# Gates by Silu with the last tile in column halves, and two chunks' row factors spread by DMA

## The chip, the cores and the metric

The kernel runs on one core of a Trainium2 chip. A core has five engines that run side by side, each with its own queue of instructions in order: TensorE (PE, matmuls), VectorE (DVE), ScalarE (ACT, activation functions from a loaded table), GpSimd (POOL) and SyncE (SP, which here only issues DMAs). TensorE writes to PSUM, eight banks of 2 KB for each of 128 partitions; the other data lie in SBUF. The metric is the device time of one execution in microseconds (us). Times inside an execution count from the start of its span, which is the time from the first to the last instruction.

## The reference

The input `x` is 2048 tokens by 512 features. All of it is computed on `xn`, the layer norm of `x`:

```python
xn = _layernorm(x)
s = _A_ref(xn, A_wqkv, A_wo)                  # windowed attention
g = _silu(_B_ref(xn, B_w1, B_w2, B_w3, B_w4))  # a mixer and an MLP
return x + s * g
```

- `_A_ref`: `q`, `k`, `v` for 32 heads of 16; token `i` attends to the eight tokens `i, i-2, ..., i-14`; softmax, weighted sum, then `@ wo`.
- `_B_ref`: `h = gelu(layernorm(xn) @ w1)`, four quarters of its columns shifted by 1, -1, 2 and -2 tokens, `@ w2`, added to `xn` as `x1`; then `x1 + gelu(layernorm(x1) @ w3) @ w4`, with 1376 hidden features.

The layer norm inside `_B_ref` is taken of `xn`, which is already normalised: its mean is zero, and it only multiplies each token by a factor, `(var * rstd**2 + eps) ** -0.5`. These are the row factors. `silu(g)` is `g * sigmoid(g)`, which equals `0.5 * g * (1 + tanh(g / 2))`.

## The kernel before

Tokens are sorted by parity, `p` = 0 (even) and 1 (odd), 1024 each, since attention with dilation 2 stays inside a parity. Each parity has two chunks of 512 tokens, so chunks 0 and 1 are parity 0, chunks 2 and 3 parity 1. A chunk has four tiles of 128 tokens, and tile `t` counts from 0 to 15. Most of SBUF is one arena, cut by hand into buffers that take turns.

The order of every engine's instructions is the order of the program's text: it is written out by hand (`manual_schedule`), and each engine's queue runs in that order. Work goes in these stages:

1. Up to about 46 us: layer norm of each chunk (`ln_stats`, `ln_norm`), its transpose (`stage_t` by TensorE for chunks 0, 1 and 3; `turn_dma` for chunk 2, a store to DRAM whose returned function issues the transposing load), the q and k projections (`qk_pair`, `qk_one`), and `stage_w1` for `h`. The moving operand of `stage_w1(c, ...)` is `xn2T[c]`, the transposed chunk times its row factors.
2. To 88 us: attention of parity 0 in units of 120 queries (`attend`: `scores`, `values`, `weighted`), with the `w2` tiles between.
3. To 126 us: `w3` with Gelu.
4. To 172 us: attention of parity 1, with the `w4` tiles of parity 0, their gates and final tiles between.
5. To the end: for each tile `t` of parity 1 a `w4_tile` (11 matmuls), its gate, and a `final_tile` one behind (4 matmuls with `wo`, times the gate, plus `x`), then stores.

**Row factors.** `ln_again(c)` computes them, a column of one value for each token with tokens on partitions: four small multiplies and an add (L345 to L347), on GpSimd except for chunk 3, and a power of -0.5 on GpSimd (L350). `stage_w1` needs them along the free axis, the same on all partitions. `stage_r(c)` does that on TensorE: four matmuls (L382) of the broadcast column with the identity, into one PSUM bank, which ScalarE copies (L386) to the last quarter of `xn2T[c]`. `stage_m(c)` (L392, VectorE) multiplies the transposed chunk by it in place. `xn2T` has two buffers, for even and odd chunks.

**PSUM.** Tags `s`, `t`, `o` have two banks each and are taken in turn by `psa`; `w` and `b` have one each, in turn by `psb`, whose counter is `cnt["b"]`. `first_t` and `stage_t` name `w` or `b` themselves. A matmul into a bank waits until the engine that reads it out is done.

**Masks and spreads.** `mask_full`, `mask_fill` (L241, L251, VectorE) write the mask's rows into the buffers of keys and queries; `spread` (L261) copies the heads' rows in by DMA, 32 of them on SP's queue from 27.88 to 50.9 us. SP's queue issues in order, and a DMA that waits holds those behind it.

**Gate and final tile.** `w4_tile` ends with an add of PSUM to `xn` on VectorE (L549). `gate(t)` is a Tanh on ScalarE (L558, `scale=0.5`) and on VectorE `(tanh + 1) * x` (L559). The missing factor 0.5 is in the attention: `v_aug` has columns of 2.0 that give twice the softmax denominator. `final_tile` multiplies PSUM by the gate (L713) and adds `x` (L715); for the tile before the last, with `act=True`, ScalarE first copies PSUM to SBUF (L712). Tables of activation functions are loaded ahead by name (`preload_act_table_set`).

Of the kernel before, what the change touches and what calls it, by code (L numbers as in the profile page):

```python
# [8 lines left out]
AF = mybir.ActivationFunctionType  # L9
ALU = mybir.AluOpType  # L10
BF16 = mybir.dt.bfloat16
# [4 lines left out]
def kernel(  # L16
# [14 lines left out]
    nc = tc.nc  # L31
    P = 128
    S = 2048
    D = 512
# [79 lines left out]
    rr_at = (184, 75)  # L114
    sg_at = (61, 66, B0 + 33.5)

    cnt = {"v": 0, "p": 0, "b": 0, "r": 0, "g": 0}

    def pst(tag, name):
        return psum.tile([P, 2 if tag in "sto" else 1, CH], F32, name=name, tag=tag)  # L120
# [209 lines left out]
    def ln_norm(c, part=slice(None)):  # L330
        p, k = c // 2, c % 2
        x_c = xn[p][:, k * TPC : (k + 1) * TPC, :]
        for lo, hi, mv, rstd in lns[c][part]:
            for j in range(lo, hi):
# [2 lines left out]
                    scalar2=rstd[:, j - lo : j - lo + 1], op0=ALU.subtract, op1=ALU.mult,  # L337
                )

    def ln_again(c):  # L340
        r2 = small.tile([P, TPC], F32, name="r2", tag="r2")
        eng = nc.vector if c == 3 else nc.gpsimd
        for lo, hi, mv, rstd in lns[c]:
            r = r2[:, lo:hi]
            eng.tensor_tensor(out=r, in0=rstd, in1=rstd, op=ALU.mult)  # L345
            eng.tensor_tensor(out=r, in0=r, in1=mv[:, :, 1], op=ALU.mult)
        eng.tensor_scalar(out=r2, in0=r2, scalar1=EPS, scalar2=None, op0=ALU.add)  # L347
        r2b = small.tile([P, TPC], BF16, name="r2b", tag="r2b")
        with nc.allow_low_precision("bf16 factors"):
            nc.gpsimd.tensor_tensor(out=r2b, in0=r2, in1=nhalf, op=ALU.pow)  # L350
# [181 lines left out]
    def w4_tile(t):  # L532
        c, jj = t // TPC, t % TPC
        p, i = c // 2, (c % 2) * TPC + jj
        st = {}

        def half(lo, hi):
            if lo == 0:
                st["pt"] = psb("w4_ps")
            pt = st["pt"]  # L540
            for ft in range(lo, hi):
                w = w4_sb[:, ft, :] if ft < NF - 1 or c < 2 else w4x_sb[:, 0, :]
                nc.tensor.matmul(  # L543
                    pt, lhsT=h3(c, ft, 1)[:, 0, jj * P : (jj + 1) * P], rhs=w,
                    start=(ft == 0), stop=(ft == NF - 1),
                )
            if hi == NF:
                x_i = xn[p][:, i, :]
                nc.vector.tensor_tensor(out=x_i, in0=pt, in1=x_i, op=ALU.add)  # L549

        return half

    def gate(t):
        c, jj = t // TPC, t % TPC
        p, i = c // 2, (c % 2) * TPC + jj
        x_i = xn[p][:, i, :]
        sig = fin.tile([P, D], BF16, name="sig", tag="f")
        nc.scalar.activation(sig, x_i, AF.Tanh, scale=0.5)  # L558
        nc.vector.scalar_tensor_tensor(out=x_i, in0=sig, scalar=1.0, in1=x_i, op0=ALU.add, op1=ALU.mult)  # L559

    orw = {}

    def values(p, u):
# [9 lines left out]
        nc.vector.tensor_copy(  # L573
            out=va[:nk, :, 0:DH], in_=vp[:nk, :].rearrange("p (h d) -> p h d", d=DH)
        )
        return va

    def scores(p, u, dd):
# [118 lines left out]
            in_=xv[p, 4 * k * P : (4 * k + 4) * P, :].rearrange("(i q) d -> q i d", q=P),  # L697
        )

    def final_tile(p, i, eng=nc.vector, ps=psb, act=False):  # L700
        pt = ps("wo_ps")
        if ps is psa:
            pt = pt[:, 0, :]
        for dt in range(ND):
            nc.tensor.matmul(  # L705
                pt, lhsT=oT[p][:, dt, i * P : (i + 1) * P], rhs=wo_sb[:, dt, :],
                start=(dt == 0), stop=(dt == ND - 1),
            )
        cnt["g"] += 1
        sg = at(sg_at[cnt["g"] % 3], 1, D)[:, 0, :]  # L710
        if act:
            nc.scalar.copy(out=sg, in_=pt)  # L712
        nc.vector.tensor_tensor(out=sg, in0=sg if act else pt, in1=xn[p][:, i, :], op=ALU.mult)  # L713
        x_o = xo[p][:, i, :]
        eng.tensor_tensor(out=x_o, in0=sg, in1=x_o, op=ALU.add)  # L715

    def store(q, p, i, n=2):
        q.dma_start(
# [225 lines left out]
    pack(1, 2)  # L944
    normalise_dn(1, 2)
    gate(7)
    for i in (0, 2, 4):
        store(nc.sync, 0, i)
    fq = [(0, 6)] + [(1, i) for i in range(6)]
    for t in range(8, 16):  # L950
        w4s[t](4 * (t == 8), NF)
        if t == 10:
            normalise_end(1, 1)
        if t == 13:
            normalise_end(1, 2)
        if t < 15:
            p, i = fq.pop(0)
            final_tile(p, i, ps=psa)
            gate(t)
            if p == 0:  # L960
                store(nc.sync, p, i, 1)
            elif i % 2:
                store(nc.sync, p, i - 1)
# [40 lines left out]
```

The softmax here doesn't subtract the row's maximum and nothing guards it: scores larger than these inputs give would overflow.

## Time and profile before

| | |
|---|---|
| median of 10 runs | 205.13 us (204.9 to 205.37) |
| the profiled execution | 205.08 us |
| its span | 203.2 us |
| TensorE matmul busy | 195.7 us, 96% of the span |
| VectorE, ScalarE, GpSimd busy | 137.2, 131.6, 74.8 us |
| stage_r: L382 (TensorE), L386 (ScalarE) | x16, 220 ns each; x4, 590 ns each |
| ln_again: L350 (GpSimd) | x4, 1172 ns each on average |
| gate: L558 (ScalarE), L559 (VectorE) | x16, 632 ns each; x16, 749 ns each |
| last steps: L713, L715 (VectorE) | 684 and 425 ns each |
| last store, issued on ACT's queue | 200.43 us |

A profile line gives the source line of the instruction, its engine, the operation and its operands; groups are followed by their count, busy time, mean duration, and the idle time of the engine just before them with what ended it. An engine that is busy all the time need not be the bound, and a wait on an engine that is not the bound costs nothing. The chain that ended last is followed back from the last instruction, at each step to what released it.

### The profile page before, as it was taken

What the parts mean: (1) busy time and instruction counts of PE and PEld (TensorE: products, weight loads), DVE (VectorE), ACT (ScalarE), POOL (GpSimd) and SP (SyncE); (2) the same over time, 40 slices, a digit from 0 to 9 for tenths busy, and PEclk for the clock granted to TensorE, in tenths of its full rate; (3) what the DMA queues carried; (4) which work ended last, traced back from release to release, by engine and by line L of the source; (5) the groups of instructions that cost most, each with busy time, mean ns of one, the idle gap of its engine ahead of it and who ended that gap; (6) DMA issues with size and microseconds to landing.
All of it is one profiled execution on the core that took longest, in us unless ns stands there. A gap on an engine that the chain in (4) does not pass through costs nothing.

```text
span 203.2 us, 4904 instructions
## 1 busy us (share of the span) xinstructions
PE 195.7 (96%) x1960; PEld 93.9 (46%) x1960; DVE 137.2 (68%) x260; ACT 131.6 (65%) x156; POOL 74.8 (37%) x151
## 2 busy tenths in 40 slices
PE   7799999999999999999999999999999999999990
PEld 2485445444444444444444444444555444444440
DVE  5788897625298998888620500288577968888874
ACT  2366778657988888895555576998788877212130
POOL 4799842200023096886770000003830590700000
PEclk9999999999999999999999999999999999999999
DMA  5992264577910079496798756793230051564212
GB/s 142 355 348 89 74 149 90 81 107 113 264 53 5 8 190 157 77 247 131 209 230 197 252 106 92 172 331 115 36 54 2 22 124 25 117 198 129 75 52 77
DMA packets 33405, 26.90 MB, mean 132 GB/s; under 512 B 14648, under 2 KB 31296, under 8 KB 33384
## 3 DMA queue, kind: packets, MB, share of 16 engines
q1 hardware_dynamic: 31192, 23.38, 44.2%
q0 software_dynamic: 2048, 3.09, 8.8%
q8 instruction: 15, 0.25, 0.6%
q10 hardware_dynamic: 144, 0.13, 0.2%
q14 instruction: 6, 0.05, 0.1%
HBM read 12.56 MB, written 4.98 MB: 86 GB/s over the span
## 4 chain that ended last, share of the span: by engine, by line
PE 84%; DVE 7%; POOL 3%; ACT 2%; issue 2%; DMA 1%; POOLq 0%
PE w_ps L543 19%; PE w_ps L506 17%; PE v_ps L569 8%; PE s_ps L589 7%; PE w_ps L464 6%; PE wo_ps L705 6%; PE qk_ps L408 5%; PE w_ps L441 5%; PE o_ps L612 4%; PE qk_ps L426 4%; PE w_ps L523 1%; DVE arena L392 1%; DVE l1s L288 1%; DMA arena<-in_A_x_dram 1%; ACT arena L594 1%
## 5 line engine op out<-in xcount | busy, mean ns | idle before, releaser
L594 ACT ACTIVATE arena<-s_ps 128x960 bf16<-128x960 f32 (+1 forms) x68 | 62.8, 976 | 13.3 <-PE s_ps L589 13.2
L543 PE MATMUL w_ps<-arena 128*128 128x512 bf16 x164 | 39.7, 380 | 0.0
L510 ACT ACTIVATE arena<-w_ps 128x1024 bf16<-128x1024 f32 x20 | 20.5, 1024 | 13.3 <-PE w_ps L506 12.6
L654 POOL DMA_DIRECT2D arena<-orw x48 | 24.8, 524 | 5.8 <-DVE orw L624 5.8
L543 PEld LDWEIGHTS <-arena 128*128 128x128 bf16 x176 | 16.5, 98 | 19.5
L715 POOL TENSOR_TENSOR arena<-arena 128x512 bf16<-128x512 bf16 x6 | 7.7, 1299 | 46.3 <-DVE arena L713 46.3
L506 PEld LDWEIGHTS <-arena 128*128 128x128 bf16 x160 | 15.5, 98 | 19.2 <-issue 0.8
L558 ACT ACTIVATE sig<-arena 128x512 bf16<-128x512 bf16 x16 | 10.1, 632 | 20.8 <-DVE arena L549 20.7
L573 DVE CAST v_aug<-v_ps 128x512 bf16<-128x512 f32 x17 | 11.7, 690 | 15.9 <-PE v_ps L569 15.9
L408 PE MATMUL qk_ps<-arena 128*128 128x512 bf16 (+1 forms) x112 | 20.5, 333 | 0.5 <-DMA arena<-in_A_wqkv_dram 0.5
L624 DVE CAST orw<-o_ps 128x960 bf16<-128x960 f32 (+1 forms) x17 | 19.7, 1157 | 1.5 <-PE o_ps L612 1.4
L549 DVE TENSOR_TENSOR arena<-w_ps,arena 128x512 bf16<-128x512 f32 x16 | 11.0, 687 | 12.0 <-PE w_ps L543 12.0
L506 PE MATMUL w_ps<-arena 128*128 128x512 bf16 x80 | 17.8, 379 | 0.1
L569 PE MATMUL v_ps<-wv_sb,arena 128*128 128x512 bf16 x68 | 17.5, 380 | 0.0
L506 PE MATMUL w_ps<-arena,arena 128*128 128x512 bf16 x80 | 17.4, 379 | 0.0
L589 PEld LDWEIGHTS <-arena 32*128 32x128 bf16 x544 | 10.2, 92 | 14.8 <-issue 14.7
L589 PE MATMUL s_ps<-arena 32*128 32x120 bf16 (+1 forms) x544 | 16.1, 213 | 0.1
L280 POOL TENSOR_SCALAR l3r<-l3m 128x1 f32<-128x1 f32 (+2 forms) x11 | 2.6, 233 | 34.9 <-DVE l3m L289 34.8
L464 PE MATMUL w_ps<-arena 128*128 128x512 bf16 x64 | 15.3, 380 | 0.0
L441 PE MATMUL w_ps<-arena 128*128 128x512 bf16 x64 | 14.8, 379 | 0.0
L408 PEld LDWEIGHTS <-arena 128*128 128x128 bf16 x112 | 10.6, 98 | 7.9 <-DMA arena<-in_A_wqkv_dram 0.8
L415 ACT CAST arena<-qk_ps 128x1024 bf16<-128x1024 f32 x11 | 11.1, 1017 | 4.5 <-PE qk_ps L408 4.5
(104 smaller groups left out, 272.8 us busy)
## 6 DMA issues: line engine op xcount, KB each, us to landing
x1n_dram<-arena SPq DMA_DIRECT2D x5, 512.0 KB, 4.2
arena<-in_A_x_dram SPq DMA_DIRECT2D x4, 512.0 KB, 6.8
arena<-in_A_x_dram SPq DMA_DIRECT2D x6, 256.0 KB, 6.5
out_dram<-arena SPq DMA_DIRECT2D x6, 256.0 KB, 2.1
arena<-in_B_w_dram SPq DMA_DIRECT2D x1, 1376.0 KB, 6.2
arena<-in_B_w_dram SPq DMA_DIRECT2D x1, 1280.0 KB
arena<-arena SPq DMA_DIRECT2D x16, 72.0 KB, 2.5
arena<-arena SPq DMA_DIRECT2D x16, 68.0 KB, 3.4
```

The costliest lines, as they stand in the source:

```text
L408: nc.tensor.matmul(pt[:, b, hh * w : (hh + 1) * w], lhsT=wqk_sb[:, dt, nt * P : (nt + 1) * P], rhs=xnT[p][:, dt, k * CH + hh * w : k * CH ...
L441: nc.tensor.matmul(pt[:, b, :], lhsT=w1_sb[:, dt, g * P : (g + 1) * P], rhs=xn2T[c][:, dt, :], start=(dt == 0), stop=(dt == ND - 1),)
L464: nc.tensor.matmul(pt, lhsT=w2_src(p, g, m0), rhs=w2_sb[:, g, :], start=(g == 0), stop=(g == ND - 1))
L506: nc.tensor.matmul(pt[:, ft % 2, :], lhsT=w3_sb[:, dt, ft * P : (ft + 1) * P], rhs=x1nT[c][:, dt, :], start=(dt == 0), stop=(dt == ND - 1),)
L510: nc.scalar.activation(h3(c, 2 * a, 2), pt, AF.Gelu_apprx_tanh)
L543: nc.tensor.matmul(pt, lhsT=h3(c, ft, 1)[:, 0, jj * P : (jj + 1) * P], rhs=w, start=(ft == 0), stop=(ft == NF - 1),)
L569: nc.tensor.matmul(vp[:nk, :], lhsT=xnT[p][:, dt, k0 : k0 + nk], rhs=wv_sb[:, dt, :], start=(dt == 0), stop=(dt == ND - 1),)
L589: nc.tensor.matmul(st[:nk, b, i * nq : (i + 1) * nq], lhsT=kT[e][r : r + 32, dt, k0 : k0 + nk], rhs=qT[e][r : r + 32, dt, q0 : q0 + nq], s ...
L594: nc.scalar.activation(prv[:nk, 2 * h : 2 * h + 2], st[:nk, :, 0 : 4 * nq], AF.Exp, scale=SCALE)
L624: nc.vector.tensor_copy(out=orw[p, r][:, :, :, q0 - ra : q0 - ra + nq], in_=op[:, :, 0 : 4 * nq].rearrange("p j (s q) -> p j s q", q=nq),)
L654: nc.gpsimd.dma_start(out=oT[p][DH * hh : DH * (hh + 1), :, ra : ra + rw], in_=orw[p, r][32 * cg : 32 * cg + DH, jj],)
L705: nc.tensor.matmul(pt, lhsT=oT[p][:, dt, i * P : (i + 1) * P], rhs=wo_sb[:, dt, :], start=(dt == 0), stop=(dt == ND - 1),)
```

## The change

Two parts.

**Row factors of chunks 1 and 2.** `stage_r(1)` and `stage_r(2)` go. The power writes its four values into column 0 of a zeroed tile `r2w` of 128 x (4 x 32). `row_turn(c)` transposes that on VectorE in blocks of 32 x 32, so that the factors lie in rows 0, 32, 64 and 96, and stores these four rows to DRAM as 512 numbers in a row (1 KB). `row_fill(c)` loads this row to all 128 partitions of the last quarter of `xn2T[c]`. All four DMAs are on SP's queue: chunk 1's two ahead of chunk 2's `turn_dma`, chunk 2's around the transposing load. The small operations of `ln_again(2)` move from GpSimd to VectorE. Since `psb` is called fewer times, `cnt["b"]` starts at 1. The order changes with it: `stage_m(1)` goes ahead of `mask_fill(0, (0,))` and of chunk 1's projections, `values(0, 0)` and `qk_pair(2, 0)` go ahead of `stage_t(3, 0)`, with the copy of the values to SBUF (`v_out`) behind it, and `ln_again(3)` goes ahead of `stage_m(2)`.

**The end.** Parity 1's gates become one Silu in place on ScalarE, with its table loaded behind the last Tanh; the final tile of parity 1 multiplies by 2.0, since a whole Silu has no half left out. Tile 15's `w4` runs in two halves of 256 columns, each with its add and gate: the first half ahead of final tile (1, 6), the second behind it; final tile (1, 7) runs in two halves as well, each in a PSUM tile of its own. (1, 6) loses its copy by ScalarE.

```diff
-    cnt = {"v": 0, "p": 0, "b": 0, "r": 0, "g": 0}
+    cnt = {"v": 0, "p": 0, "b": 1, "r": 0, "g": 0}
...
+    r2w = small.tile([P, TPC, 32], BF16, name="r2w", tag="r2w", bufs=1)
+    nc.vector.memset(r2w[:], 0.0)
+
+    def row_turn(c):
+        turned = small.tile([P, TPC, 32], BF16, name=f"r2t{c}", tag="r2t", bufs=1)
+        nc.vector.transpose(
+            out=turned.rearrange("q t i -> q (t i)"), in_=r2w.rearrange("q t i -> q (t i)")
+        )
+        row = dram.tile([TPC, P], BF16, name=f"r2_d{c}")
+        nc.sync.dma_start(
+            out=row.rearrange("t (g i) -> g t i", g=4),
+            in_=turned[0:P:32],
+        )
+        r2s[c] = row
+
+    def row_fill(c):
+        nc.sync.dma_start(
+            out=xn2T[c][:, ND - 1, :],
+            in_=r2s.pop(c).rearrange("t q -> (t q)").unsqueeze(0).to_broadcast([P, CH]),
+        )
...
-        eng = nc.vector if c == 3 else nc.gpsimd
+        eng = nc.vector if c >= 2 else nc.gpsimd
...
-        r2b = small.tile([P, TPC], BF16, name="r2b", tag="r2b")
+        if c in (1, 2):
+            r2b = r2w[:, :, 0]
+        else:
+            r2b = small.tile([P, TPC], BF16, name="r2b", tag="r2b")
...
-        def half(lo, hi):
+        def half(lo, hi, ds=slice(0, D)):
...
-    def gate(t):
+    def gate(t, ds=slice(0, D)):
         c, jj = t // TPC, t % TPC
         p, i = c // 2, (c % 2) * TPC + jj
-        x_i = xn[p][:, i, :]
+        x_i = xn[p][:, i, ds]
+        if p:
+            nc.scalar.activation(x_i, x_i, AF.Silu)
+            return
...
-    def final_tile(p, i, eng=nc.vector, ps=psb, act=False):
...
+    def final_tile(p, i, eng=nc.vector, ps=psb, halves=1):
...
+        n = D // halves
+        for lo in range(0, D, n):
+            ds = slice(lo, lo + n)
+            pt = ps("wo_ps")
+            pt = (pt[:, 0, :] if ps is psa else pt)[:, 0:n]
...
+            if p:
+                nc.vector.scalar_tensor_tensor(
+                    out=sg[:, ds], in0=pt, scalar=2.0, in1=x_i[:, ds], op0=ALU.mult, op1=ALU.mult
+                )
+            else:
+                nc.vector.tensor_tensor(out=sg[:, ds], in0=pt, in1=x_i[:, ds], op=ALU.mult)
+            eng.tensor_tensor(out=x_o[:, ds], in0=sg[:, ds], in1=x_o[:, ds], op=ALU.add)
...
     stage_t(1, 1)
+    row_turn(1)
+    row_fill(1)
     ln_stats(2, 2, 4)
     mask_full(0)
     ln_norm(2)
-    turn_dma(2)()
+    turn = turn_dma(2)
     ln_again(2)
     stage_w1(0, 1)
     mask_full(1)
+    row_turn(2)
+    turn()
+    row_fill(2)
+    stage_m(1)
     mask_fill(0, (0,))
     for a in range(2):
         qk_pair(1, a)[0]()
-    stage_r(1)
-    stage_m(1)
     ln_stats(3, 0, 2)
...
     stage_w1(1, 1)
-    stage_r(2)
+    va, v_out = values(0, 0, True)
+    qk_pair(2, 0)[0]()
     stage_t(3, 0)
+    v_out()
     ln_norm(3, slice(1, 2))
+    ln_again(3)
     stage_m(2)
-    ln_again(3)
-    qk_pair(2, 0)[0]()
     stage_t(3, 1)
...
     nc.scalar.preload_act_table_set("exp_and_others")
-    va = values(0, 0)
...
     gate(7)
+    nc.scalar.preload_act_table_set("silu_and_others")
...
-    for t in range(8, 16):
+    for t in range(8, 15):
...
     final_tile(0, 7, ps=psa)
     store(nc.sync, 0, 7, 1)
-    gate(15)
-    final_tile(1, 6, ps=psa, act=True)
+    halves = [slice(a, a + D // 2) for a in (0, D // 2)]
+    w4s[15](0, NF, halves[0])
+    gate(15, halves[0])
+    final_tile(1, 6, ps=psa)
     store(nc.sync, 1, 6, 1)
-    final_tile(1, 7, ps=psa)
+    w4s[15](0, NF, halves[1])
+    gate(15, halves[1])
+    final_tile(1, 7, ps=psa, halves=2)
     store(nc.scalar, 1, 7, 1)
```

More of the change, by code (lines that the diff above doesn't have):

```diff
@@ L535, in w4_tile @@
         st = {}
-        def half(lo, hi):
+        def half(lo, hi, ds=slice(0, D)):
             if lo == 0:
                 st["pt"] = psb("w4_ps")
-            pt = st["pt"]
+            pt = st["pt"][:, ds]
             for ft in range(lo, hi):
-                w = w4_sb[:, ft, :] if ft < NF - 1 or c < 2 else w4x_sb[:, 0, :]
+                w = w4_sb[:, ft, ds] if ft < NF - 1 or c < 2 else w4x_sb[:, 0, ds]
                 nc.tensor.matmul(
@@ L547, in half @@
             if hi == NF:
-                x_i = xn[p][:, i, :]
+                x_i = xn[p][:, i, ds]
                 nc.vector.tensor_tensor(out=x_i, in0=pt, in1=x_i, op=ALU.add)
         return half
-    def gate(t):
+    def gate(t, ds=slice(0, D)):
         c, jj = t // TPC, t % TPC
         p, i = c // 2, (c % 2) * TPC + jj
-        x_i = xn[p][:, i, :]
+        x_i = xn[p][:, i, ds]
+        if p:
+            nc.scalar.activation(x_i, x_i, AF.Silu)
+            return
         sig = fin.tile([P, D], BF16, name="sig", tag="f")
@@ L561, with values @@
     orw = {}
-    def values(p, u):
+    def values(p, u, later=False):
         q0, nq, k0, nk = units[u]
@@ L572, in values, with evict @@
             )
-        nc.vector.tensor_copy(
-            out=va[:nk, :, 0:DH], in_=vp[:nk, :].rearrange("p (h d) -> p h d", d=DH)
-        )
+        def evict():
+            nc.vector.tensor_copy(
+                out=va[:nk, :, 0:DH], in_=vp[:nk, :].rearrange("p (h d) -> p h d", d=DH)
+            )
+        if later:
+            return va, evict
+        evict()
         return va
@@ L698, in load_xo @@
         )
-    def final_tile(p, i, eng=nc.vector, ps=psb, act=False):
[L701 to L708, printed above, removed]
+    def final_tile(p, i, eng=nc.vector, ps=psb, halves=1):
         cnt["g"] += 1
         sg = at(sg_at[cnt["g"] % 3], 1, D)[:, 0, :]
[L711 to L715, printed above, removed]
+        x_i, x_o = xn[p][:, i, :], xo[p][:, i, :]
+        n = D // halves
[3 more added lines that the diff above has]
+            pt = (pt[:, 0, :] if ps is psa else pt)[:, 0:n]
+            for dt in range(ND):
+                nc.tensor.matmul(
+                    pt, lhsT=oT[p][:, dt, i * P : (i + 1) * P], rhs=wo_sb[:, dt, ds],
+                    start=(dt == 0), stop=(dt == ND - 1),
+                )
+            if p:
+                nc.vector.scalar_tensor_tensor(
+                    out=sg[:, ds], in0=pt, scalar=2.0, in1=x_i[:, ds], op0=ALU.mult, op1=ALU.mult
+                )
+            else:
+                nc.vector.tensor_tensor(out=sg[:, ds], in0=pt, in1=x_i[:, ds], op=ALU.mult)
+            eng.tensor_tensor(out=x_o[:, ds], in0=sg[:, ds], in1=x_o[:, ds], op=ALU.add)
     def store(q, p, i, n=2):
@@ L955 @@
             normalise_end(1, 2)
[L956 to L963, printed above, removed]
+        p, i = fq.pop(0)
+        final_tile(p, i, ps=psa)
+        gate(t)
+        if p == 0:
+            store(nc.sync, p, i, 1)
+        elif i % 2:
+            store(nc.sync, p, i - 1)
         if t == 10:
```

## The prediction

> **What bounds the kernel now.** I read the page first: share of busy time, then the chain that ended last.
>
> ```profile
> PE 195.7 (96%) x1960; PEld 93.9 (46%) x1960; DVE 137.2 (68%) x260; ACT 131.6 (65%) x156; POOL 74.8 (37%) x151
> ...
> PE 84%; DVE 7%; POOL 3%; ACT 2%; issue 2%; DMA 1%; POOLq 0%
> ```
>
> TensorE (PE) is busy from the first loads to the end and makes 84% of the chain. So time is won only where PE's own work shrinks, where PE waits, or after its last matmul. The list of PE's waits has four entries, three of them at the start; the fourth is the only one that the change touches:
>
> ```profile
> PE rrep_ps L382 <- POOL r2b L350: 0.3, 1, 0.3
> ```
>
> The chain around it, start and length in us, says who is late: VectorE (DVE) ends L347, GpSimd (POOL) ends the pow (L350) only 2.1 us later, and the next matmul of any kind stands behind it.
>
> ```profile
> 34.49 0.18 DVE r L347
> ...
> 34.71 0.44 issue
> 35.15 1.58 POOL r2b L350
> 36.73 0.05 issue
> 36.78 0.40 PE rrep_ps L382 x4
> ```
>
> The end of the same chain is no longer PE's: after the last tiles seven VectorE instructions stand in a row.
>
> ```profile
> 195.89 0.88 PE wo_ps L705 x4
> ...
> 196.79 0.70 DVE arena L713
> ...
> 197.52 0.43 DVE arena L715
> 197.94 0.60 DVE arena L559
> 198.54 0.35 DVE arena L713
> ...
> 198.91 0.42 DVE arena L715
> 199.34 0.61 DVE arena L713
> ...
> 199.98 0.43 DVE arena L715
> ```
>
> PE's last matmul ends at about 198.5 (two more groups of four after 196.77, at 0.86 each), VectorE at 200.41; the last store takes the rest to 203.2.
>
> Last, the timelines of VectorE and GpSimd (start, length) around 24 us, for what blocks a GpSimd instruction:
>
> ```profile
> 23.25 0.68 DVE L241 TENSOR_TENSOR arena<-arena,edge 128x512 bf16<-128x512 bf16 x1
> 23.86 1.29 DVE L251 COPY arena<-arena 128x2048 bf16<-128x2048 bf16 x2
> ```
>
> ```profile
> 23.47 0.53 POOL L346 TENSOR_TENSOR r<-r,l1m 128x2 f32<-128x2 f32 x1
> 24.08 1.10 POOL L347 TENSOR_SCALAR r<-r 128x4 f32<-128x4 f32 x1
> ```
>
> L346 (0.2 alone) ends at 24.00, just behind the tensor_tensor L241. L347 (0.23 elsewhere) ends at 25.18, just behind both copies: it was held through two copies, but L346 got in between a tensor_tensor and a copy.
>
> **What the Trainium skill says.** "SBUF — State Buffer", Who interferes with whom: a VectorE copy in a two-port mode, or a tensor_tensor with two SBUF inputs, shuts GpSimd's reads out for the whole instruction. The trace agrees (above; also L280, 1.19 against 0.22, beside L392). "VectorE: DVE Perf Modes", The three transpose paths: 311 ns for a 128x128 bf16 transpose in 32x32 blocks; no run here shows one. "ScalarE: Activation LUTs", What ACT_TABLE_LOAD costs: all functions cost the same per element, and a table switch is 1283 ns plus a 1380 ns drain. The trace has 1.28 at L807 with the first Exp 0.01 behind, so no drain. "DMA: Bandwidth & Descriptors", Latency and other measured facts: a fixed cost of about 2 us per DMA; the small stores of L666 took 1.5 to 3.1.
>
> **The change, first part: row factors.** Removed from PE: stage_r(1) and stage_r(2), 0.22 each in issue time (the chain has 0.22 for x4 at 12.44), 0.44 in all. values(0,0) only moves: its 0.86 leaves 45.65 and fills 30.7 to 31.55. The old wait also ends if the pow comes in time. PE's issue of L441 ended at about 36.35, the rrep began at 36.78: 0.43. Most that this part can give: 0.87. Also removed are two ScalarE copies L386 (0.6 each), worth nothing since ScalarE waits for PE there.
>
> Added: two VectorE transposes (0.25 of queue time each, from 311 ns less overlap), four DMAs on SP's queue, ln_again(2)'s five small operations moved from POOL to VectorE (0.8, from 33.84 to 34.66 for chunk 3), and one memset before 2 us.
>
> - Row of chunk 1: the pow ended at 18.68, the transpose goes at 19.4 behind copy L363, the store at 19.7. Store 1.5 to 3.1 and fill 2.3 to 3.7 (the landings of L261's queue) give 23.5 to 26.5 us; the DMA engines are idle from 18 to 24 (share 0.01 and 0.00). stage_m(1) asks for it at about 26.2. Nothing, most likely.
> - VectorE behind: ln_norm(2) ends 0.27 later, 23.5; ln_again(2) 24.35; mask_full(1) 24.93. It is a tensor_tensor of two SBUF inputs, so the pow (1.04) runs from 24.9 to 25.95. VectorE must wait for that in row_turn(2), and stage_m(1), mask_fill and the statistics of chunk 3 stand behind it. Transpose to 26.25, stage_m(1) (1.23) to 27.45. PE, 0.22 early, asks for it at 27.23, before it was 27.45. **A new wait of 0.27.** Bounds: 0 if the pow isn't held, 0.8 if it takes 1.57 as at 35.15.
> - turn() of chunk 2 stands on SP behind row_turn(2)'s store (26.1 + 0.39), and needs its own first store, 26.5 against 26.28. The chunk's 256-byte packets moved from 27.76 to 30.14; now about 0.3 later. qk_pair(2,0) asks at 31.56 plus 0.27, because values(0,0) went in front: 1.3 of cover; without it the 0.3 would be paid. row_fill(2) is issued at about 28.3 and lands behind these by 31.5; stage_m(2) starts at 34.4. The spreads start 0.8 later, and the second eight wait for mask_fill anyway (36.8 against 35.86): issued by 41.7, landed by 44.2 (2.5), asked for by the first scores at about 46.
> - Chunk 3: from stage_m(1) on, VectorE: two copies 1.22, statistics 3.2, ln_norm 0.65, v_out 0.6, to 33.05; ln_norm of the other half to 33.7 (stage_t(3,1) asks at 34.0: 0.3 spare), ln_again(3) to 34.43. Then stage_m(2), a tensor_tensor, to 35.57 and two copies to 36.8. The pow for stage_r(3) is released at 34.5 and held by stage_m(2). If it gets in behind that, as L346 did, it ends at 36.65, or 36.85 if the write waits for the copies; PE asks at 36.76 + 0.27 = 37.03: no wait. If the copies hold it too, as they did L347, it ends at 37.65 to 37.9: a wait of 0.6 to 0.9. I take the first, since the tensor_tensor stands first in the row.
>
> Sum: 0.87 - 0.27 = 0.60 us won; ends 0.87 and -0.3. PE has no other wait until the end, so this is carried there.
>
> **Second part: the end.** Seven gates lose the VectorE multiply (0.68) in the loop, worth nothing: VectorE waits for PE there (0.6 before L549). The table load (1.28, or 2.66 by the skill) stands at 171.6 in ScalarE's 2.5 us of idle time before 174.12; even the longer one delays only a gate whose result is needed at 177. Silu costs what Tanh did (0.63).
>
> The order on PE is now (0,7), first half of w4(15), (1,6), second half, (1,7) in halves. PE's sum doesn't change: the 128x256 matmuls of L408 come at 0.109 (x16 in 1.75), so 22 of them 2.40 against 2.37. In the old clock: half one ends at 195.6, (1,6) 196.45, half two 197.65, (1,7) 198.09 and 198.52. A half-width VectorE operation from PSUM: 512 columns take 0.69 and 960 take 1.157, so 1.04 ns a column and 0.15 fixed, 0.42 for 256; the add from SBUF 0.28 (224 columns took 0.268 at L687). Half a Silu: 512 take 0.63 and 1024 take 1.02, so 0.44.
>
> VectorE: (1,6) 196.48 to 197.63; second half added 197.69 to 198.1; Silu to 198.55; (1,7) first half 198.12 to 198.54 and its add to 198.86; second half 198.8 to 199.22 and add to 199.53. Before: 200.41. **Won: 0.88.** Bounds: nothing if a half costs as much as a whole, 1.1 if the adds overlap better. The act copy of (1,6) goes away inside this.
>
> Sum: 0.60 + 0.88 = 1.48. The profiled execution took 205.08, 203.2 of it span and 1.88 around it; it becomes 203.6 (span 201.7). The median, 205.13, stands 0.05 above: 203.65.
>
> **The rivals.** (B) GpSimd is shut out longer: both copies hold the pow for stage_r(3), or the first pow runs 0.5 longer, and the front gives -0.3 to 0.1. For it: L347 and the 2.1 us of the old pow. Against it: L346. 0.88 - 0.1 gives 204.35. (C) The halves don't pay because the fixed part of each VectorE and ScalarE step is larger behind a semaphore; against it, L687's 0.268. Tail 0.2: 204.3. (E) No new wait at all: 0.87 + 1.0, 203.25. (D) Slower: row_fill(1) lands late. stage_m(1) stands on it, with PE right behind, and each us past 26.2 costs one us. Store plus fill must take 8.4 us rather than 4 to 7 to eat the 1.48 and another 0.41; the engines' idle share speaks against it, the largest landing of that queue (6.0) for it. At 9 us: 205.7. (F) The change does nothing measurable, if the front loses what the end wins: -0.8 in front, 205.1.
>
> **How the numbers follow.** A no-change measurement can't be told from 0.2%, 0.41 us. Chances: likeliest (203.65, own range 203.3 to 204.0) 0.48; B 0.25; C 0.08; E 0.08; D 0.06; F 0.05. From 203.2 (E) to 204.7 (the worse end of B and C) leaves out D, F and some of E, under 0.2. Faster: the first four, 0.89, less a little of B and C beyond 204.72: 0.87. Same: F and that little: 0.06. Slower: 0.07.
>
> **What would show it.** Right: no L382 for chunks 1 and 2; L441 for chunk 1 waiting about 0.3 for L392; no wait at the one remaining L382 after 36; first scores 0.6 earlier (46.6 to 46.0); VectorE's last add 1.0 us behind PE's end rather than 1.9. Wrong: DMA as releaser of stage_m(1), a PE wait over 0.5 at stage_r(3), or a last VectorE row that still takes 0.69 per half.

## The result, and the profile after

The changed kernel takes 203.55 us (median of nine runs, 203.50 to 204.79) where the kernel before takes 205.17 (31 runs beside it). The ratio is 0.9928, 95% interval 0.9918 to 0.9938: 1.62 us less by the medians, 1.27 to 1.68 by that interval of 205.17. The forecast was 203.65. Two of the nine runs of one kernel below, after_late, lie more than 1.5% above its fastest and are left out of its numbers.

The profiled execution is one of those that take longer: 204.49 us, 202.7 of it span, 0.94 above the median, because TensorE waits once in its middle. The times of most other executions leave no room for that wait. No profile of such an execution of this kernel was taken; those of after_pad and after_store6 below, at 203.53 and 203.55 us, lose less than 0.2 us at that place.

The page of the changed kernel, share of busy time and the chain that ended last:

```profile
PE 195.6 (96%) x1967; PEld 95.1 (47%) x1967; DVE 134.1 (66%) x263; ACT 131.4 (65%) x155; POOL 73.6 (36%) x146
...
PE 76%; DMA 10%; DVE 6%; POOL 5%; issue 2%; POOLq 0%; DVEq 0%
```

TensorE is as busy as before. But a tenth of the chain is now DMA (1% before), and the list of TensorE's waits says where it enters:

```profile
PE warm_ps L176 <- DVE ones_bf L167: 1.0, 1, 1.0
PE w_ps L530 <- DMA arena<-x1n_dram: 0.7, 1, 0.7
PE tr_ps L327 <- DVE arena L319: 0.5, 1, 0.5
PE qk_ps L432 <- ACT arena L328: 0.4, 1, 0.4
```

The old wait for the powers (L382, 0.3) is gone. In its place stands one that the prediction did not have: L530, the first w3 matmul on chunk 1, waits until 96.9 us for the transposing load of that chunk's normalised rows. The list counts 0.7 from the modelled end of the matmul before; from start to start the row of matmuls is 0.9 us longer there.

The front part, in the chain between 34 and 38 us: chunk 3's row factors (L406) follow w1 without a gap.

```profile
36.20 0.86 PE w_ps L465 x4
37.06 0.22 PE rrep_ps L406 x4
```

VectorE's timeline around 24 us (start, length, in brackets the idle time before): mask_full(1) (L241), the transpose of row_turn(2) (L345), stage_m(1) (L416).

```profile
24.21 0.69 DVE L241 TENSOR_TENSOR arena<-arena,edge 128x512 bf16<-128x512 bf16 x1
25.81 0.31 DVE L345 STREAM_TRANSPOSE r2t<-r2w 128x128 bf16<-128x128 bf16 x1 [0.91 <-POOL r2w L374]
26.05 1.18 DVE L416 TENSOR_TENSOR arena<-arena 128x2048 bf16<-128x2048 bf16 x1
```

GpSimd's timeline, the powers of chunks 2 and 3:

```profile
24.38 1.39 POOL L374 TENSOR_TENSOR r2w<-r,nhalf 128x4 bf16<-128x4 f32 x1 [1.59 <-DVE r L368]
...
34.43 2.30 POOL L374 TENSOR_TENSOR r2b<-r,nhalf 128x4 bf16<-128x4 f32 x1 [1.59 <-DVE r L368]
```

VectorE stands idle for 0.91 us until the first of these is done, as foreseen, and stage_m(1) comes right behind the transpose, so chunk 1's spread row was there in time. The transpose took 0.31 us; the Trainium skill ("VectorE: DVE Perf Modes", The three transpose paths) has 311 ns for this shape, and the trace agrees.

The end of the chain:

```profile
196.39 0.70 DVE arena L747
...
197.12 0.42 DVE arena L752
197.54 0.40 DVE arena L573
...
198.03 0.44 DVE arena L747
...
198.52 0.40 issue
198.92 0.44 DVE arena L747
...
199.38 0.29 DVE arena L752
```

The gates' multiplies on VectorE are gone from this row, and the halves cost 0.44 and 0.29 as worked out. Ahead of the second half's multiply, though, the chain has 0.40 us in which nothing that the profile shows is waited for (the first half's add runs until 198.78 beside it). TensorE's last matmul ends at 198.35, VectorE at 199.67: 1.3 behind, not 1.0.

### The profile page after: what moved, and what is told of

Read it like the earlier page. It is cut to its first block, busy times and chain, and to the rows that moved or that the text cites. A ratio compares the mean times of both kernels' runs of the same rounds, so it can differ in the third digit from the quotient of the medians.

```text
span 202.7 us, 4914 instructions
## 1 busy us (share of the span) xinstructions
PE 195.6 (96%) x1967; PEld 95.1 (47%) x1967; DVE 134.1 (66%) x263; ACT 131.4 (65%) x155; POOL 73.6 (36%) x146
## 4 chain that ended last, share of the span: by engine, by line
PE 76%; DMA 10%; DVE 6%; POOL 5%; issue 2%; POOLq 0%; DVEq 0%
PE w_ps L567 19%; PE w_ps L530 13%; PE qk_ps L432 9%; PE w_ps L465 7%; PE wo_ps L742 6%; PE v_ps L596 6%; PE s_ps L621 5%; PE w_ps L488 4%; DMA x1n_dram<-arena 3%; PE o_ps L644 3%; DMA arena<-orw 3%; DMA arena<-x1n_dram 3%; PE qk_ps L450 2%; POOL arena L686 1%; PE w_ps L547 1%
## 5 line engine op out<-in xcount | busy, mean ns | idle before, releaser
L626 ACT ACTIVATE arena<-s_ps 128x960 bf16<-128x960 f32 (+1 forms) x68 | 62.8, 976 | 12.3 <-PE s_ps L621 12.3
L567 PE MATMUL w_ps<-arena 128*128 128x512 bf16 (+1 forms) x173 | 40.1, 369 | 0.0
L567 PEld LDWEIGHTS <-arena 128*128 128x128 bf16 x187 | 17.6, 98 | 18.9
L530 PEld LDWEIGHTS <-arena 128*128 128x128 bf16 x160 | 15.4, 98 | 20.2 <-DMA arena<-x1n_dram 1.2
L573 DVE TENSOR_TENSOR arena<-w_ps,arena 128x512 bf16<-128x512 f32 (+1 forms) x17 | 11.2, 659 | 14.9 <-PE w_ps L567 14.9
L582 ACT ACTIVATE arena<-arena 128x512 bf16<-128x512 bf16 (+1 forms) x9 | 5.2, 583 | 20.4 <-DVE arena L573 20.4
L530 PE MATMUL w_ps<-arena,arena 128*128 128x512 bf16 x80 | 17.4, 379 | 0.7 <-DMA arena<-x1n_dram 0.7
L530 PE MATMUL w_ps<-arena 128*128 128x512 bf16 x80 | 17.8, 379 | 0.1
L488 PE MATMUL w_ps<-arena 128*128 128x512 bf16 x64 | 15.3, 380 | 0.0
L492 DVE TENSOR_TENSOR arena<-w_ps,arena 128x512 bf16<-128x512 f32 x16 | 10.4, 684 | 7.2 <-PE w_ps L488 7.2
L465 PE MATMUL w_ps<-arena 128*128 128x512 bf16 x64 | 14.8, 379 | 0.0
```

Of the source, the lines that this page charges most:

```text
L465: nc.tensor.matmul(pt[:, b, :], lhsT=w1_sb[:, dt, g * P : (g + 1) * P], rhs=xn2T[c][:, dt, :], start=(dt == 0), stop=(dt == ND - 1),)
L488: nc.tensor.matmul(pt, lhsT=w2_src(p, g, m0), rhs=w2_sb[:, g, :], start=(g == 0), stop=(g == ND - 1))
L530: nc.tensor.matmul(pt[:, ft % 2, :], lhsT=w3_sb[:, dt, ft * P : (ft + 1) * P], rhs=x1nT[c][:, dt, :], start=(dt == 0), stop=(dt == ND - 1),)
L567: nc.tensor.matmul(pt, lhsT=h3(c, ft, 1)[:, 0, jj * P : (jj + 1) * P], rhs=w, start=(ft == 0), stop=(ft == NF - 1),)
L626: nc.scalar.activation(prv[:nk, 2 * h : 2 * h + 2], st[:nk, :, 0 : 4 * nq], AF.Exp, scale=SCALE)
```

## The experiments

All were timed in five rounds beside the kernel before, which stood between 205.19 and 205.32 us. What settles most questions is where the profiled executions of all kernels stand at five points. In us:

- A: from the transposing matmuls of chunk 0's fourth tile (10.3 us, behind TensorE's first waits; two expectations call them the second four of tile 0) to the first scores
- B: on to the first w3 matmul
- C: on to the first scores of parity 1
- D: on to the end of VectorE's last add
- F: from the last store's landing (1.77 to 1.79 behind D in all of them) to the end of SP's row of looks at the transfers (its second DRAIN, at 201.96 in the changed kernel)
- G: on to the end of the span
- H: time less span

| kernel | median | A | B | C | D | F | G | H |
|---|---|---|---|---|---|---|---|---|
| before | 205.17 | 36.31 | 41.21 | 38.08 | 74.51 | 0.27 | 0.77 | 1.88 |
| after | 203.55 | 35.52 | 40.90 | 38.99 | 73.94 | 0.51 | 0.77 | 1.76 |
| front_only | 204.15 | 35.52 | 40.89 | 38.08 | 74.50 | 0.51 | 0.76 | 1.77 |
| tail_only | 204.27 | 36.31 | 41.21 | 38.07 | 73.70 | 0.27 | 0.77 | 1.95 |
| rows_pe | 204.40 | 35.86 | 41.21 | 38.08 | 73.70 | 0.27 | 0.99 | 2.11 |
| whole_end | 204.15 | 35.52 | 40.89 | 38.08 | 74.17 | 0.51 | 0.99 | 1.78 |
| after_late | 206.98 | 35.52 | 40.89 | 38.91 | 76.47 | 0.51 | 0.77 | 1.77 |
| after_store6 | 203.27 | 35.52 | 40.89 | 38.25 | 73.93 | 0.15 | 0.77 | 1.77 |
| after_pad | 203.47 | 35.51 | 40.89 | 38.20 | 73.70 | 0.51 | 0.77 | 1.78 |
| after_mask | 203.81 | 35.65 | 40.89 | 39.81 | 73.93 | 0.51 | 0.77 | 1.77 |
| best | 203.50 | 35.65 | 40.89 | 39.37 | 73.61 | 0.14 | 0.77 | 1.77 |
| three | 203.02 | 35.52 | 40.89 | 38.97 | 73.61 | 0.15 | 0.77 | 1.76 |

A to H of each row are of one profiled execution. The stretches repeat to 0.02 us from kernel to kernel wherever the same cause acts, so a difference of 0.1 can be read; C also has the wait at L530, which differs from execution to execution. None of the kernels leaves work of the computation out.

**The two parts alone (front_only, tail_only).** First the new front part with the old gates, final tiles and order of the end, as edits of the changed kernel; then the reverse, as edits of the kernel before.

```diff
...
-        if p:
-            nc.scalar.activation(x_i, x_i, AF.Silu)
-            return
...
-    nc.scalar.preload_act_table_set("silu_and_others")
...
-    for t in range(8, 15):
+    for t in range(8, 16):
...
-    final_tile(1, 7, ps=psa, halves=2)
+    final_tile(1, 7, ps=psa)
```

```diff
...
+        if p:
+            nc.scalar.activation(x_i, x_i, AF.Silu)
+            return
...
+    nc.scalar.preload_act_table_set("silu_and_others")
...
-    for t in range(8, 16):
+    for t in range(8, 15):
...
-    final_tile(1, 7, ps=psa)
+    final_tile(1, 7, ps=psa, halves=2)
```

> The row-factor part alone, with the gates and the end as before. The prediction's step: 0.60 us won, 204.55. Theory after the first profile: 1.0 us won up to 87 us less a small wait at L530 for chunk 1, 204.2 to 204.5. Rival (the end carries everything): 205.1.

> The end alone (Silu gates, halves), with the row factors and the order at the front as before. The prediction's step: 0.88 us won, 204.25. By the first profile VectorE ends 1.31 us behind TensorE's last matmul where it was 1.9 before, so 0.6 won: 204.55. Rival (the halves don't pay): 205.0.

Measured: 204.15 us, ratio 0.9944 (0.9924 to 0.9964), and 204.27, ratio 0.9944 (0.9923 to 0.9964). The front part wins 0.79 in A and 0.32 in B and loses 0.24 in F. The end wins 0.81 in D and nothing elsewhere. In the whole change D has only 0.57, so the 0.24 that is missing comes neither from the front part nor from the end alone, but from their being in one program.

**The change again, and GpSimd's spreads moved (after_again, after_spread).** The first theory of the wait at L530 was GpSimd's queue: eight spreads of parity 1 stand there ahead of the statistics of tiles 5 to 7. They were put behind those.

```diff
-        late[3 + 2 * w].append(lambda w=w: spread(1, 0, CUT, nc.gpsimd, (w,)))
+        late[5].append(lambda w=w: spread(1, 0, CUT, nc.gpsimd, (w,)))
```

> The changed kernel once more, for a second profile. In the first one TensorE waited 0.74 us at the w3 matmuls of chunk 1 (L530) for the transposed chunk from DRAM, and that execution took 204.49 against a median of 203.55. Theory (the front is worth about 1.0 us by 87 us, and this wait takes back a varying part of it): an execution near 203.55 shows a wait there of under 0.3 us, first scores at 45.9 and the first w3 matmul at 86.7. Rival (the wait is always there, and the long execution has another cause): a wait of 0.7 us at 203.5 too.

> The changed kernel with the first eight spread DMAs of parity 1 issued by GpSimd two units later, behind the statistics of tiles 5 to 7, so that these (released at 79.0, run at 83.6 in the first profile) are not held behind them. Theory (the chunk is late for w3 because its normalisation waits for GpSimd's queue): no wait at L530 for chunk 1, and 203.4 or less, with no execution above 204. Rival (the DMA engines' load makes it late): the same wait and 203.55 as before.

Measured: 203.68 us, ratio 0.9920 (0.9900 to 0.9941), and 203.90, ratio 0.9927 (0.9903 to 0.9950). The profile of after_again fell on a long execution again (204.47 us) and has the wait, 0.61, so it does not show what a short execution looks like. The wait was 0.77 in after_spread, though there the store was issued at 84.66, 0.45 earlier than in the changed kernel, and landed at 91.75, no earlier than its 91.72. It is not the queue: this theory fell.

**All sixteen of GpSimd's spreads far later (after_late).** This takes load off the DMA engines between 80 and 92 us.

```diff
-    for w in range(2):
-        late[3 + 2 * w].append(lambda w=w: spread(1, 0, CUT, nc.gpsimd, (w,)))
...
                 pack(0, 2)
+                spread(1, 0, CUT, nc.gpsimd)
```

> The changed kernel with all 16 of GpSimd's spreads of parity 1 (eight of them issued around 80 to 90 us) moved behind the last pack, near 105 us. Theory: the DMA load of these spreads delays chunk 1's normalised store, which landed 6.6 us after its issue, and so the transposing load that TensorE waits for at its first w3 matmul of chunk 1 (0.61 to 0.77 us in the changed kernel): the wait is gone, parity 1's scores start near 125.1 instead of 125.7, and a profiled execution takes 203.8 to 204.1 instead of 204.5 us; the median falls by up to 0.5, to 203.1 to 203.6. Rival: the load is that of other transfers (the loads of weights, the value spreads on SP): the store lands as late as before, the wait stays at 0.6 to 0.8 and the time at 203.5 to 203.7. Second rival: the spreads come too late for their readers, and TensorE waits for them in the scores of parity 1: over 204.

Measured: 206.98 us, ratio 1.0085 (1.0057 to 1.0113). The landings of the normalised stores (two in each kernel, that of chunk 1 the longer), in the changed kernel:

```profile
DMA to landing us min/median/max: 4.3/5.4/6.6
```

and in this one:

```profile
DMA to landing us min/median/max: 3.8/4.2/4.5
```

The transposing load landed at 93.31 rather than 96.87, and the wait at L530 is gone: the load that these spreads put on the DMA engines is what makes chunk 1 late, as the theory had it. Why one execution of the same kernel has the wait and another does not is not shown. The second rival is right as well, at other readers than it named. The waits that came instead:

```profile
PE wo_ps L742 <- DMA arena<-in_A_wo_dram: 1.9, 1, 1.9
...
PE v_ps L596 <- DVE arena L573: 0.6, 1, 0.6
...
PE w_ps L547 <- DMA arena<-x1n_dram: 0.4, 1, 0.4
```

The first two make up the 2.53 us by which D is longer than in the changed kernel. SP issued the load of `wo` at 135.5 us here and at 128.0 in the changed kernel; what held it was not followed up.

**The row factors by TensorE again (rows_pe).** The new order, the values brought forward and the new end are kept.

```diff
...
-    row_turn(1)
-    row_fill(1)
...
-    row_turn(2)
     turn()
-    row_fill(2)
-    stage_m(1)
...
+    stage_r(1)
+    stage_m(1)
     ln_stats(3, 0, 2)
...
     stage_w1(1, 1)
+    stage_r(2)
```

> The changed kernel with the row factors of chunks 1 and 2 made by TensorE again (matmuls and copies of stage_r), and everything else of the change kept: order of work, values brought forward, end. Theory: what the rows' new way saves is TensorE's 0.44 us of matmuls, less the 0.10 us that TensorE still waits for the last multiply of chunk 1; the first scores, at 45.85 us in the changed kernel, come at 46.1 to 46.3. Four transfers fewer are issued by SP, so the last store's semaphore is again the last that is looked at and 0.25 us of that comes back at the end: 203.6 to 203.9 us in all. Rival: the reordering alone carries the gain of the front part, and the first scores stay at 45.8 to 45.9: 203.3 to 203.5. Second rival: the copies by VectorE are late and TensorE waits over 0.5 us at the first chunks: first scores at 46.6 or later, over 204.1.

Measured: 204.40 us, ratio 0.9960 (0.9948 to 0.9972), 0.5 above what the theory gave. Its mechanism is right: the first scores come at 46.18, A is 0.34 longer than in the changed kernel, which is 0.44 less 0.10. So of A's 0.79, 0.34 are the rows'; the other 0.45, what is left, fit the end of the old wait. The rest came from places that it had not looked at: against the changed kernel B is 0.31 longer, G 0.22 and H 0.35, and D 0.24 shorter.

B first. ScalarE's timeline at the place where B differs: the exponentials (L594, L626 in the changed kernel) behind scores of parity 0, before

```profile
61.52 1.83 ACT L594 ACTIVATE arena<-s_ps 128x960 bf16<-128x960 f32 x2 [0.82 <-PE s_ps L589]
```

and after

```profile
60.45 1.83 ACT L626 ACTIVATE arena<-s_ps 128x960 bf16<-128x960 f32 x2 [0.51 <-PE s_ps L621]
```

The same wait for the same scores lasts 0.31 longer before. The trace shows what it is made of: ScalarE has seen the semaphore at 61.17 and starts at 61.52; its starts elsewhere in this stage follow in some 0.05. And 0.66 behind that start an instruction fetch of 8 KB begins. In tail_only and rows_pe it is the same recorded instruction of ScalarE, its 64th. So I read this as ScalarE crossing into a new block of its program. In the kernels with fewer copies on ScalarE ahead, this place has no gap. No run moves ScalarE's instructions alone, so this reading is argued and not tested.

**The last tile whole (whole_end).**

```diff
-    for t in range(8, 15):
+    for t in range(8, 16):
...
-    w4s[15](0, NF, halves[0])
-    gate(15, halves[0])
+    gate(15)
     final_tile(1, 6, ps=psa)
     store(nc.sync, 1, 6, 1)
-    w4s[15](0, NF, halves[1])
-    gate(15, halves[1])
-    final_tile(1, 7, ps=psa, halves=2)
+    final_tile(1, 7, ps=psa)
```

> The changed kernel with its last tile whole: one Silu of 512 columns, one multiply and one add for tile 15, w4 of it in order; the front part and Silu kept. Theory: the halves take a half multiply, a half add and a half Silu off the chain behind TensorE's end; of the 0.58 us that VectorE's end came nearer to the third of the scores with the changed end, Silu alone (one multiply for two instructions) keeps about a third, so the last add ends 0.3 to 0.45 us later against the start of parity 1's scores (74.2 to 74.4 us behind it, where the changed kernel shows 73.93 and the kernel before 74.52): 203.9 to 204.1 us. Rival: the halves pay nothing, since the second multiply starts late and each half has a fixed cost: 73.9 to 74.0 us and 203.5 to 203.6.

Measured: 204.15 us, ratio 0.9955 (0.9941 to 0.9970). D is 74.17: Silu alone wins 0.34, and the halves 0.23 more as the changed kernel has them, or 0.47 as tail_only has them. The last two operations now have the full lengths:

```profile
197.95 0.68 DVE L747 SCALAR_TENSOR_TENSOR arena<-wo_ps,arena 128x512 bf16<-128x512 f32 x1
198.67 0.42 DVE L752 TENSOR_TENSOR arena<-arena 128x512 bf16<-128x512 bf16 x1
```

The rival falls. G is again 0.22 longer than elsewhere: VectorE's own part in the closing handshake of the engines begins 0.49 behind its release instead of 0.11. This kernel and rows_pe have an instruction fetch 0.68 behind that stop, and the changed kernel has one 0.68 behind its 0.40 at 198.92. In all three the instruction concerned is number 319 among VectorE's recorded ones, counted from nought. The kernel before has 318 of them in all. The number is not the same in every kernel: front_only's last fetch, at 192.92, lies near its number 312, and none follows its 319.

**Twelve idle instructions on VectorE (after_pad).** If this reading is right, adding work must make the kernel faster.

```diff
+    idle = small.tile([P, 1], F32, name="idle", tag="idle", bufs=1)
...
+        if t in (9, 11):
+            for k in range(6):
+                nc.vector.memset(idle, 0.0)
         if t == 10:
```

> The changed kernel with twelve one-column memsets of an unused tile added on VectorE, six behind the final tile of turn t = 9 and six behind that of t = 11, where VectorE stands idle for about 1.16 us; nothing is left out. Theory: the 0.40 us that VectorE takes before the last half multiply (0.17 in the kernel with the changed end alone) is the crossing into a new block of its program: in four traces an instruction fetch follows 0.68 us behind such a stop at VectorE's 319th recorded instruction, and the kernel before ends at 318. Twelve instructions more move the crossing to where VectorE idles, the gap falls to 0.17 and VectorE's end comes 73.7 us behind the start of parity 1's scores instead of 73.93: 203.2 to 203.4 us. Rival: the gap belongs to the semaphores of the half multiply, and stays at 0.40; the memsets cost nothing or delay the gates: 203.5 to 203.8 us.

Measured: 203.47 us, ratio 0.9905 (0.9887 to 0.9923). The changed kernel's 0.9928 lies just above that interval, but its own interval overlaps it, and 203.47 stands between the theory's 203.2 to 203.4 and the rival's 203.5: the total does not decide. The profile does. The chain at its end:

```profile
197.75 0.03 DVE arena L752
197.78 0.17 issue
197.96 0.43 DVE arena L747
...
198.41 0.29 DVE arena L752
```

0.17 in place of 0.40, D at 73.70, and the fetch has moved to 193.8 us, where VectorE is at work on multiplies and adds that follow each other without a gap of that kind. The 0.24 that the change lost between its parts is this stop, by all signs the crossing: front_only has nine recorded instructions of VectorE more than the kernel before and, if its fetch at 192.92 is VectorE's, crosses near 192.3 us, where VectorE waits for TensorE anyway; tail_only has two fewer and does not come to the crossing; with both, it falls on the last half tile.

**Three stores as one (after_store6).** F is longer in every kernel with the four new transfers of the rows.

```diff
-    for i in (0, 2, 4):
-        store(nc.sync, 0, i)
+    store(nc.sync, 0, 0, 6)
```

> The changed kernel with parity 0's first three stores of two tiles each as one store of six tiles, two transfers fewer on SP before the last stores. Theory: SP looks at the transfers' semaphores one after another at the end, some 0.06 us for each pair, and the last store's stands fourth or fifth from the end in the changed kernel, so that the program ends 0.50 us after its landing; two transfers fewer put it last, and 0.2 to 0.35 us are won: 203.2 to 203.4 us, with the last store landing where it did. Rival: the looks follow the landing whatever the order and what counts is the landing alone: unchanged, 203.5 to 203.7. Second rival: the one large store holds the rings when the last tiles' stores are due, and the last landing comes later: 203.7 or more.

Measured: 203.27 us, ratio 0.9918 (0.9900 to 0.9937). F is 0.15 and the last landing stands where it did behind D. SP looks at the transfers' semaphores two by two, 0.06 us a step, in a fixed order, and the last store stands elsewhere in it with each transfer more or less: in the changed kernel it is seen at 201.46 and the last look comes at 201.96, with seven steps between (six pairs of transfers and a DRAIN); here one step is left. The theory holds.

**The mask later (after_mask).**

```diff
-    mask_full(1)
     row_turn(2)
     turn()
     row_fill(2)
     stage_m(1)
+    mask_full(1)
```

> The changed kernel with parity 1's mask table (mask_full(1), 0.69 us on VectorE beside GpSimd's powers of chunk 2) moved behind stage_m(1). Theory: while VectorE makes the mask, GpSimd's power is held; without it the power of chunk 2 takes 1.04 instead of 1.39 us, the fill and stage_m(1) come 0.3 us earlier, and TensorE's 0.10 us in front of stage_w1(1,0) goes: first scores 35.4 us behind the second four transposes of tile 0's start (35.52 in the changed kernel), 203.4 to 203.5 us. Rival: the power's time is its own, 1.39 us, and nothing changes: 203.5 to 203.6. Second rival: the mask comes too late behind stage_m(1), or holds the multiplies of a later chunk, and TensorE waits there: over 203.7.

Measured: 203.81 us, ratio 0.9926 (0.9907 to 0.9946). GpSimd's timeline:

```profile
24.37 1.02 POOL L374 TENSOR_TENSOR r2w<-r,nhalf 128x4 bf16<-128x4 f32 x1 [1.59 <-DVE r L368]
...
34.65 2.30 POOL L374 TENSOR_TENSOR r2b<-r,nhalf 128x4 bf16<-128x4 f32 x1 [1.59 <-DVE r L368]
```

Without the mask beside it the power takes 1.02 rather than 1.39, and TensorE goes into stage_w1(1,0) without its 0.10. But the mask now pushes VectorE's later work, chunk 3's power ends at 36.95 instead of 36.73, and TensorE, which would be there at 36.77, waits 0.24 for it. A is 0.13 longer: the second rival. The median lies 0.26 above the changed kernel's; more executions with the wait at L530 (1.6 us in the profiled one) may be the rest, which is not shown.

**All together, and without the mask's move (best, three).** The last tile's adds are one in both:

```diff
             else:
                 nc.vector.tensor_tensor(out=sg[:, ds], in0=pt, in1=x_i[:, ds], op=ALU.mult)
-            eng.tensor_tensor(out=x_o[:, ds], in0=sg[:, ds], in1=x_o[:, ds], op=ALU.add)
+        eng.tensor_tensor(out=x_o, in0=sg, in1=x_o, op=ALU.add)
```

> The changed kernel with the store of six tiles (two transfers fewer), twelve idle memsets on VectorE, parity 1's mask table behind stage_m(1), and the last tile's two half adds as one add of 512 columns behind both half multiplies. Theory: the four add up: about 0.30 us from the order of the semaphores at the end, 0.23 from VectorE's program block, 0.10 from the mask, 0.07 from the add (0.42 for one behind the multiplies, where a half add holds the second multiply by 0.21 and 0.29 follows): 202.8 to 203.0 us. Rival: only the semaphores' part is real: 203.2 to 203.3 us.

> The changed kernel with the store of six tiles, twelve idle memsets on VectorE and the last tile's adds as one, and with parity 1's mask table where the change has it. Theory: the mask's move made TensorE wait 0.24 us for row factors of chunk 3 and is what cost the run with all four; without it the first scores are again 35.5 us behind the second four transposes of tile 0, VectorE's end comes 73.6 us behind the start of parity 1's scores, SP's last looks take 0.15 instead of 0.50 us: 202.8 to 203.1 us where TensorE does not wait for chunk 1's transposed data, and 0.9 more in an execution where it does. Rival: the larger store or the lone add delays the last landing, and the time stays at 203.4 or more.

Measured: 203.50 us (203.02 to 204.44), ratio 0.9910 (0.9887 to 0.9933), for all four, which misses the theory's 202.8 to 203.0: the mask's move costs 0.13 in A instead of winning 0.10, and three of the six executions took 203.8 us or more. For three: 203.02 us (202.88 to 203.79), ratio 0.9892 (0.9875 to 0.9908), as its theory had it. The single add brings D to 73.61, 0.09 less. With the mask where the change has it, A is 35.52 again. The last kernel is the fastest of this study: 0.5 below the changed kernel by the medians, 2.2 below the one before, and its interval lies below that of the changed kernel. In both, the profiled execution has the wait at L530 (0.7 in three, 1.1 in best).

## Why the prediction came true, and where its steps did not

The total was 0.10 off; its terms were further off and cancelled, so that the number came out so close is in part luck. It had 0.60 in front and 0.88 at the end, 1.48. An execution of the changed kernel without the wait at L530 would have, by the table, 0.79 (A) + 0.32 (B) + 0.57 (D) - 0.24 (F) = 1.44, and 0.12 in H, whose cause I did not find. That makes 1.56, against 1.62 of the medians.

- **The matmuls of stage_r and the old wait: 0.87, right.** rows_pe shows 0.34 for the rows, which is 0.44 less the new wait, and leaves 0.45 for the rest, where the prediction had 0.43.
- **The new wait of 0.27: mis-sized, it is 0.10.** The place and the cause were right. I let the power run from 24.9, behind the mask; it started at 24.38 beside it and was held for part of its time (1.39 where 1.02 is its own), so it ended at 25.77 rather than 25.95, and the transpose overlapped with stage_m(1).
- **The power of chunk 3: right.** It was put at 36.65, or 36.85 if its write waits for VectorE's two copies; it ended at 36.73, just behind them (36.69), released at 34.43 (34.5 foreseen), 2.30 us in all. TensorE began those matmuls at 36.90 (37.03 foreseen). Rival B falls, but by 0.17 us of slack, as after_mask shows.
- **Row of chunk 1 and rival D: right.** Store and fill were there before 26.05; no multiply waited for a DMA. The 205.7 that the prediction gives for a row at 9 us is a slip of its sum: 2.5 us late on 203.65 would be 206.15. Nothing rests on it.
- **"PE has no other wait until the end, so this is carried there": the step that failed.** In the kernel before, TensorE came to chunk 1's first w3 matmul at 97.09, and the transposed rows had landed at 96.91. This margin of 0.2 us stands in no list of waits. TensorE now comes 1.1 earlier; the load landed at 95.5 in front_only's profile, where TensorE went on at 95.97, and at 96.87 in the changed kernel's. So some executions lose some 0.9 us, and with it the gain of the front part. The first matmuls, before and after:

```profile
97.09 17.43 PE L506 MATMUL w_ps<-arena,arena 128*128 128x512 bf16 x80
```

```profile
96.91 17.44 PE L530 MATMUL w_ps<-arena,arena 128*128 128x512 bf16 x80 [0.74 <-DMA arena<-x1n_dram]
```

- **The end, 0.88: the mechanism right, the size 0.81 alone and 0.57 in the changed kernel.** Silu alone gives 0.34, the halves the rest, against rival C. The 0.07 fit the start of the multiplies that read TensorE's result and wait for ScalarE too: in the changed kernel they start 0.1 behind it (196.29 to 196.39, 197.93 to 198.03), where the prediction had 0.03. The other 0.24 are VectorE's stop, read as its crossing into a new block.
- **The last store: -0.24, not foreseen.** The four added transfers moved the last store forward in the order in which SP looks.
- **B's 0.32, not foreseen**, and as large as the error in the other direction. The prediction put the two removed copies on ScalarE at nothing; in rows_pe, which brings them back, B is 41.21 again. Without this gain the forecast would have been 0.2 too low by the medians.

Rival E (no new wait, 203.25) is nearest in front: 0.79 of its 0.87.

## What to carry to other kernels

Removing a wait early in the kernel is worth what the next transfer lets through: look in the trace for how long each later operand had been there when it was first used, since a margin of 0.2 us is in no list of waits. When a part is timed alone and together, and the gains do not add, compare stretches between fixed points of the traces; here that separated causes of 0.1 to 0.3 us which the medians only hint at. Counts of instructions and of transfers can move the end by a quarter of a us each, whatever the instructions do.

## What the runs showed of the hardware that was not expected

- **Program blocks.** A stop that I read as an engine's step into a new block of its instructions cost 0.23 us (VectorE, 0.40 against 0.17) to 0.31 (ScalarE, 0.82 against 0.51) where nothing hid it; a fetch of 8 KB follows 0.64 to 0.68 us later. The Trainium skill ("Runtime: NRT & Kernel Launch", Instruction fetch mechanics) says that an engine fetches its next block while it works on the present one, and that a crossing costs little and is mostly hidden. The traces show it hidden in after_pad, and not in the changed kernel. That the stop is this crossing is inferred from the fetches, from the instruction's number in three kernels (front_only does not fit it), and, for VectorE alone, from the twelve memsets that moved it.
- **The end of the program.** SP's looks at the transfers take 0.06 us for each pair, 0.14 to 0.51 in all behind the last landing, by where the last store stands in the order.
- **GpSimd beside VectorE.** The same power of 128x4 values took 1.02 us alone, 1.39 where a 0.69 us tensor_tensor ran beside it, and 2.30 where a tensor_tensor and two copies did.
- **Left open.** What lies around the span is 1.76 to 1.78 us in most kernels, but 1.88 before, 1.95 in tail_only and 2.11 in rows_pe.
